# Routed attention with a GELU block on one core: the row-sum check one turn later, and operands of later batches prepared closer to their use

## The chip, the core and the metric

One core of a Trainium2 chip runs the whole program. The metric is device time in microseconds (us). Engines are named as in the profile: PE is TensorE (PEld its weight loads), DVE is VectorE, ACT is ScalarE, POOL is GpSimd, SP issues most DMAs. L409 is line 409 of the kernel before. Each engine takes its instructions strictly in the order in which the program writes them.

## The reference

For 4 batches, 8 heads, 768 positions and width 64, queries and keys are each given to the nearest of 16 centroids of their head; a query attends only to keys with the same centroid. The result goes through two matrix products with a quick GELU between them.

```
q_assign = np.argmax(np.einsum('bhsd,hcd->bhsc', q_n, c_n), axis=-1)
k_assign = np.argmax(np.einsum('bhsd,hcd->bhsc', k_n, c_n), axis=-1)
mask = q_assign[:, :, :, None] == k_assign[:, :, None, :]
scores = np.where(mask, scale * np.matmul(q, k.transpose(0, 1, 3, 2)), -1e9)
attn = softmax(scores);  x = (attn @ v) as (B*S, H*D) = (3072, 512)
h = x @ w_in                      # 512 -> 2048
out = (h * sigmoid(1.702 * h)) @ w_out
```

The arrays come as 64-bit floats. q, k and v are read as 32-bit; the two weight matrices are rounded on the chip.

## The kernel before

**Units and turns.** The heads are taken in pairs: 16 pairs p, four to a batch. A group g is one pair and one half (384) of its queries; groups run batch by batch, first half of the queries for pairs 0 to 3, then second half. A group has six units u, one for each 128 keys. The main loop runs over turns t of two units each: three turns to a group, 24 to a batch, 96 turns and two more to drain. Scheduling is manual: what the loop writes is the order on every engine.

**One turn** writes, in this order:

1. `scores(u)` (L384, PE) for its two units into two PSUM buffers `s`; for batch 0 `part(u)` (L398) adds the mask by a small matmul. Both `s` buffers must have been released by the exponentials of the turn before.
2. `exps(u)` (L409, ACT).
3. From turn 12 on (`second`), one `round_next()`.
4. `mask(u)`: DVE L420 from batch 1 on; POOL adds the exponentials up in `sum` (L430).
5. `prep_near` of a pair, where it is due; then `values(u)` (L441, PE) for the units of the turn before, and at a group's end a copy of the result to `x` (L446, ACT).
6. In every third turn (4, 7, 10, ...) `normalise(g)`: ones matmul over `sum` (L453, PE), reciprocal (L456, DVE), product with x (L458, DVE). From turn 12 on it stands ahead of the other preparation steps, before that behind them.
7. The other preparation steps of this turn.
8. `check(g)`: two ACT passes over the reciprocals (L468, L470), whose row sums tell at the end whether this fast path was valid. It overwrites the reciprocals, so it waits for L458.
9. `round_next()` in most turns; then pieces of the second block; and in odd turns from 12 on one more `round_next()`.

**Rounding of weights.** 32 pieces of 128x512 come by DMA (`raw`, 512 KB, three buffers, L146). A round has two DVE operations (L159, L161), two of ACT on their results (L163, L165), and three more of DVE for the piece before (L171, L174, L177). Rounds run in turns 1 to 21; before turn 12 none is written at the end of turns 3, 7 and 11.

**Preparation of a pair** has seven steps, one for a turn in batches 1 to 3 and two for a turn in batch 0:

- steps 0 to 3, `prep_turn`: three transposes (L262, PE) into a PSUM bank, and a copy to `T` (L267, ACT). Step 0 also loads v (L120); steps 1 and 3 also take the next q or k load from a queue (L111, three buffers).
- step 4, `prep_near`: four small matmuls (L276) and a copy (L282, ACT).
- step 5, `prep_assign`: transposes (L287, PE) and five DVE operations (L293 to L316).
- step 6, `prep_spread`: one transpose (L323), a copy (L328, ACT), and two DMAs (L330, L332) that spread the codes to all partitions as `qb`. For batch 0 this step is `prep_hot` (L349, with evictions L354 and L356).

**The second block** for a half batch is 16 `first` (four 128x128 by 384 products, each written as two passes, L487; tanh L492 on ACT; product L494 on DVE) and then 12 `second` (four products, L504; every fourth one evicts `y`, L510, ACT, and stores it). They are taken at a rate of about 2.4 for a turn from turn 14 on. All short PSUM tiles of preparation, normalisation and second block (`m`) share three banks; a `y` holds one of them over several pieces.

The lines that place the steps of later batches:

```
            elif b == 0:
                t = (hp - 2) * TG + 1 + i // 2
            else:
                t = b * TB + (-20, -8, -2, 1)[hp] + i
            prep_at.setdefault(t, []).append((p, i))
```

Of the kernel before, what the change touches and what calls it, by code (L numbers as in the profile page):

```python
# [18 lines left out]
def kernel(  # L19
    tc: tile.TileContext,  # L20
    q: bass.AP,
    k: bass.AP,
    v: bass.AP,
    centroids: bass.AP,
    moe_w_in: bass.AP,
    moe_w_out: bass.AP,
    out: bass.AP,
):

    args = (q, k, v, centroids, moe_w_in, moe_w_out, out)
    bad = fast(tc, *args)
    with tc.If(bad > 0):
        general(tc, *args)
# [3 lines left out]
def fast(  # L39
# [142 lines left out]
    def round_next():  # L182
        i = w_done[0]
        if i < NW:
            load_w(i + 2)
            split_w(i)
        if 0 < i <= NW:
            join_w(i - 1)
        w_done[0] += 1
# [183 lines left out]
    def split(g):  # L373
        b, r = divmod(g, 2 * HP)
        h, hp = divmod(r, HP)
        return b * HP + hp, h

    def scores(u):
        g, kt = divmod(u, NJ)
        p, h = split(g)  # L380
        ps = ps_s.tile([P, 2, 512], FP32, name="s")
        for a in range(2):
            rows = slice(a * D, (a + 1) * D)
            nc.tensor.matmul(out=ps[:, a, 0:HALF],  # L384
                             lhsT=T[p, 1][rows, kt * P:(kt + 1) * P],
                             rhs=T[p, 0][rows, h * HALF:(h + 1) * HALF],
                             start=True, stop=(p >= HP))
        s_of[u] = ps[:, :, 0:HALF]

    def part(u):  # L390

        g, kt = divmod(u, NJ)
        p, h = split(g)
        if p >= HP:
            return
        for a in range(2):
            r = 32 * (2 * (p % 2) + a)
            nc.tensor.matmul(  # L398
                out=s_of[u][:, a, :],
                lhsT=hots[p // 2, 1][r:r + NC, kt * P:(kt + 1) * P],  # L400
                rhs=hots[p // 2, 0][r:r + NC, h * HALF:(h + 1) * HALF],
                start=False, stop=True)

    def exps(u):
        p, h = split(u // NJ)
        s = s_of[u]
        if p < HP:
            A_of[u] = ap.tile([P, 2, HALF], FP32, name="A")
        nc.scalar.activation(out=A_of[u] if p < HP else s, in_=s, func=AF.Exp,  # L409
                             scale=SCALE)  # L410

    def mask(u):

        g, kt = divmod(u, NJ)
        p, h = split(g)
        s = s_of.pop(u)
        if p >= HP:
            A_of[u] = ap.tile([P, 2, HALF], FP32, name="A")
            for a in range(2):
                nc.vector.scalar_tensor_tensor(  # L420
                    out=A_of[u][:, a, :],
                    in0=qcode[p][:, a, h * HALF:(h + 1) * HALF],
                    scalar=code[p][:, kt % NH, 1, kt // NH, a:a + 1],
                    in1=s[:, a, :], op0=ALU.is_equal, op1=ALU.mult)
        A = A_of[u]
        if kt == 0:
            return
        if kt == 1:
            sum_of[g] = ap.tile([P, 2, HALF], FP32, name="sum", bufs=2)
        nc.gpsimd.tensor_tensor(out=sum_of[g],  # L430
                                in0=A_of[u - 1] if kt == 1 else sum_of[g],
                                in1=A, op=ALU.add)

    def values(u):
        g, kt = divmod(u, NJ)
        p, h = split(g)
        if kt == 0:
            o_of[g] = ps_o.tile([P, 512], FP32, name="o")
        A = A_of.pop(u)
        for a in range(2):  # L440
            nc.tensor.matmul(out=o_of[g][a * D:(a + 1) * D, 0:HALF],  # L441
                             lhsT=v_in[p][:, a, kt, :], rhs=A[:, a, :],
                             start=(kt == 0), stop=(kt == NJ - 1))
        if kt == NJ - 1:
            O_of[g] = xp.tile([P, HALF], FP32, name="x")
            nc.scalar.copy(O_of[g], o_of.pop(g)[:, 0:HALF])  # L446

    def normalise(g):

        sm = sum_of.pop(g)  # L450
        ps = bank()
        for a in range(2):
            nc.tensor.matmul(out=ps[a * D:(a + 1) * D, 0:HALF], lhsT=ones,  # L453
                             rhs=sm[:, a, :], start=True, stop=True)
        rec = recs[g] = short()
        nc.vector.reciprocal(out=rec, in_=ps[:, 0:HALF])  # L456
        x = xT_of[g] = O_of.pop(g)
        nc.vector.tensor_tensor(out=x, in0=x, in1=rec, op=ALU.mult)  # L458
        if g % HP == HP - 1:
            ffn.extend(ffn_chunks(g // HP))  # L460

    recs = {}

    def check(g):


        rec = recs.pop(g)
        nc.scalar.activation(out=rec, in_=rec, func=AF.Copy,  # L468
                             accum_out=sums[:, 0, g:g + 1])
        nc.scalar.activation(out=rec, in_=rec, func=AF.Relu, bias=top[:, 0:1],  # L470
                             scale=-2.0 * LIMIT * LIMIT,
                             accum_out=sums[:, 1, g:g + 1])
# [51 lines left out]
    TB = 2 * HP * TG  # L524

    prep_at = {}
    for p in range(1, NPAIR):
        b, hp = divmod(p, HP)
        for i in range(2 if p == 1 else 0, len(PREP)):
            if p == 1:  # L530
                t = (i - 2) // 2
            elif b == 0:
                t = (hp - 2) * TG + 1 + i // 2
            else:
                t = b * TB + (-20, -8, -2, 1)[hp] + i
            prep_at.setdefault(t, []).append((p, i))
    loads = deque((p, w) for p in range(NPAIR) for w in range(2))
    for _ in range(3):
# [2 lines left out]
    def prep(p, i):  # L541
        if i == 0 and p:
            load_v(p)
        PREP[i](p)
        if i in (1, 3) and loads:
            load_qk(*loads.popleft())
# [7 lines left out]
    for t in range(NT + 2):  # L554
        us = range(2 * t, 2 * t + 2) if t < NT else ()
        for u in us:
            scores(u)
        if t == 0:
            prep(0, 6)
        for u in us:  # L560
            part(u)
        for u in us:
            exps(u)
        second = t >= TB // 2
        if second:
            round_next()
        for u in us:
            mask(u)
        work = sorted(prep_at.get(t, ()), key=lambda w: PREP[w[1]] != prep_near)
        while work and PREP[work[0][1]] == prep_near:  # L570
            prep(*work.pop(0))
        if 1 <= t <= NT:
            for u in range(2 * t - 2, 2 * t):
                values(u)
        owed = owed + rate if ffn else 0.0
        g = (t - 2) // TG if t >= 2 and (t - 2) % TG == TG - 1 else None
        if g is not None and second:
            normalise(g)
        for p, i in work:
            prep(p, i)  # L580
        if g is not None and not second:
            normalise(g)
        if recs:
            check(*recs)
        if second or t and t % 4 != 3:
            round_next()
        while owed >= 1 and ffn:
            ffn.popleft()()
            owed -= 1
        if second and t % 2:  # L590
            round_next()


    ok = const.tile([P, 2, 2 * NPAIR], FP32, name="ok")
    nc.vector.tensor_scalar(out=ok, in0=sums, scalar1=LIMIT, scalar2=None,
# [457 lines left out]
```

## Time and profile before

| | us |
|---|---|
| median of 3 runs (1087.89 to 1088.94) | 1088.09 |
| profiled execution | 1089.2 |
| its span, first to last instruction | 1087.3 |
| PE busy / DVE / ACT / POOL in the span | 1049.0 / 490.8 / 354.8 / 296.9 |
| ACT idle until L458 ahead of L468 (32 times) | 111.2 |
| PE idle until L409 ahead of L384 (5 times) | 9.6 |

Lines of the timeline give start, duration, engine, line, operation, output and input, shapes and count; in brackets stands the idle time of the engine before it, and who ended it. Neighbouring instructions of one form are merged. Turns are found by their scores: turn 4 starts on PE at 34.80 us, turn 10 at 69.33, turn 12 at 82.10, turn 16 at 118.78, turn 20 at 168.65, turn 25 at 229.57, turn 46 at 450.54.

### The profile page before, as it was taken

Reading aid. Unit: us, or ns where it says so; the run is one execution under the profiler, and the core shown is the slowest. Engines: PE = TensorE matmul, PEld = TensorE weight load, DVE = VectorE, ACT = ScalarE, POOL = GpSimd, SP = SyncE. Lnnn points to the kernel's source line nnn. Section 1 sums busy time; section 2 is a strip of 40 time slices with the busy share of each in tenths; the row PEclk is TensorE's granted clock in tenths of the full one; section 3 lists DMA queues with packets and bytes.
Section 4 is the critical chain, followed back from the end, with each engine's and each line's share of the span. In section 5 each row is a group of like instructions: output and inputs, shape, how many; then the busy total and the mean of one; then the engine's idle time right before and its main releaser. Section 6 shows DMA issues by size and latency. Waiting matters only on the chain. (4 is left out here: it accounts for less than half of the span.)

```text
span 1087.3 us, 10456 instructions
## 1 busy us (share of the span) xinstructions
PE 1049.0 (96%) x3982; PEld 492.6 (45%) x3982; DVE 490.8 (45%) x744; ACT 354.8 (33%) x665; POOL 296.9 (27%) x168
## 2 busy tenths in 40 slices
PE   7878799999999999999999999999999999999997
PEld 3423344445544455444454445444554445444543
DVE  3889999225442344424453164423552344431200
ACT  3755555223422333223432233223332133311100
POOL 2644223213232333123231142222332333230000
PEclk9998899999999999999999999999999999999999
DMA  7623443110100010002100000010000000000000
GB/s 199 165 81 116 131 133 111 46 49 17 49 23 27 10 30 15 31 25 54 51 23 17 15 20 15 15 48 32 8 7 12 10 10 1 1 10 20 1 11 22
DMA packets 64813, 45.13 MB, mean 42 GB/s; under 512 B 51953, under 2 KB 57585, under 8 KB 64753
## 3 DMA queue, kind: packets, MB, share of 16 engines
q1 hardware_dynamic: 64608, 44.33, 14.3%
q8 instruction: 33, 0.54, 0.2%
q14 instruction: 28, 0.22, 0.1%
q10 hardware_dynamic: 144, 0.03, 0.0%
HBM read 38.04 MB, written 6.31 MB: 41 GB/s over the span
## 5 line engine op out<-in xcount | busy, mean ns | idle before, releaser
L430 POOL TENSOR_TENSOR sum<-sum,A 128x768 f32<-128x768 f32 x128 | 235.5, 1840 | 461.3 <-DVE A L420 364.1
L487 PE MATMUL m<-x,w_in 128*128 128x384 f32 x1024 | 347.1, 494 | 9.7 <-ACT T L267 4.4
L504 PE MATMUL m<-w_out,g 128*128 128x512 f32 x768 | 337.8, 594 | 0.7 <-ACT short L282 0.7
L420 DVE SCALAR_TENSOR_TENSOR A<-qb,code,s 128x384 f32<-128x384 uint8 x288 | 157.6, 609 | 274.6 <-ACT s L409 251.9
L487 PEld LDWEIGHTS m<-x,w_in 128*128 128x128 f32 x1024 | 192.2, 192 | 149.1 <-issue 16.3
L504 PEld LDWEIGHTS m<-w_out,g 128*128 128x128 f32 x768 | 143.3, 190 | 175.6 <-issue 171.5
L494 DVE SCALAR_TENSOR_TENSOR g<-g,m 128x384 f32<-128x384 f32 x128 | 70.0, 553 | 220.4 <-ACT g L492 220.3
L384 PE MATMUL s<-T,T 64*128 64x384 f32 x768 | 152.9, 517 | 9.7 <-ACT A L409 9.6
L409 ACT ACTIVATE s<-s 128x768 f32<-128x768 f32 x144 | 107.9, 792 | 136.0 <-PE s L384 136.0
L441 PE MATMUL o<-A,inv 128*64 128x384 f32 x768 | 146.3, 502 | 0.0
L492 ACT ACTIVATE g<-m 128x384 f32<-128x384 f32 x128 | 61.7, 487 | 196.4 <-PE m L487 196.3
L430 POOL TENSOR_TENSOR sum<-A 128x768 f32<-128x768 f32 x32 | 60.0, 1876 | 215.6 <-DVE A L420 179.5
L384 PEld LDWEIGHTS s<-T,T 64*128 64x128 f32 x768 | 66.6, 189 | 94.6 <-issue 52.2
L456 DVE RECIPROCAL short<-m 128x384 f32<-128x384 f32 x32 | 81.6, 2551 | 25.8 <-PE m L453 25.8
L441 PEld LDWEIGHTS o<-A,inv 128*64 128x64 f32 x768 | 46.8, 137 | 84.8 <-issue 84.1
L510 ACT ACTIVATE y<-m 128x512 f32<-128x512 f32 x24 | 14.3, 595 | 155.8 <-PE m L504 142.7
L468 ACT ACTIVATE short<-short 128x384 f32<-128x384 f32 x32 | 16.7, 523 | 111.2 <-DVE x L458 111.2
L409 ACT ACTIVATE A<-s 128x768 f32<-128x768 f32 x48 | 36.1, 804 | 22.0 <-PE s L398 22.0
L267 ACT COPY T<-m 128x384 f32<-128x384 f32 x64 | 29.7, 480 | 37.2 <-PE m L262 37.1
L262 PE MATMUL m<-ident,in 128*128 128x128 f32 x192 | 33.9, 298 | 3.1 <-ACT T L267 1.7
L163 ACT ACTIVATE e<-e,low 128x512 int32<-128x512 int32 x32 | 23.1, 722 | 28.8 <-DVE e L159 28.8
L262 PEld LDWEIGHTS m<-ident,in 128*128 128x128 f32 x192 | 21.5, 146 | 22.4 <-issue 11.9
(68 smaller groups left out, 373.5 us busy)
## 6 DMA issues: line engine op xcount, KB each, us to landing
raw<-in_moe_w_in_dram SPq DMA_DIRECT2D x16, 512.0 KB
raw<-in_moe_w_out_dram SPq DMA_DIRECT2D x16, 512.0 KB
in<-in_q_dram SPq DMA_DIRECT2D x32, 192.0 KB
in<-in_k_dram SPq DMA_DIRECT2D x32, 192.0 KB
inv<-in_v_dram SPq DMA_DIRECT2D x16, 384.0 KB
out_dram<-y SPq DMA_DIRECT2D x24, 256.0 KB
qb<-line SPq DMA_DIRECT2D x12, 192.0 KB
line<-row SPq DMA_DIRECT2D x12, 1.5 KB
```

The costliest lines, as they stand in the source:

```text
L262: nc.tensor.transpose(out=ps[:, n * P:(n + 1) * P], in_=qk_in[p, w][:, h * NH + n].rearrange("p a d -> p (a d)"), identity=ident)
L267: nc.scalar.copy(dst, ps[:, 0:HALF])
L384: nc.tensor.matmul(out=ps[:, a, 0:HALF], lhsT=T[p, 1][rows, kt * P:(kt + 1) * P], rhs=T[p, 0][rows, h * HALF:(h + 1) * HALF], start=True, ...
L409: nc.scalar.activation(out=A_of[u] if p < HP else s, in_=s, func=AF.Exp, scale=SCALE)
L420: nc.vector.scalar_tensor_tensor(out=A_of[u][:, a, :], in0=qcode[p][:, a, h * HALF:(h + 1) * HALF], scalar=code[p][:, kt % NH, 1, kt // NH ...
L430: nc.gpsimd.tensor_tensor(out=sum_of[g], in0=A_of[u - 1] if kt == 1 else sum_of[g], in1=A, op=ALU.add)
L441: nc.tensor.matmul(out=o_of[g][a * D:(a + 1) * D, 0:HALF], lhsT=v_in[p][:, a, kt, :], rhs=A[:, a, :], start=(kt == 0), stop=(kt == NJ - 1))
L456: nc.vector.reciprocal(out=rec, in_=ps[:, 0:HALF])
L487: nc.tensor.matmul(out=ps[:, 0:HALF], lhsT=w_in[:, c, f * P:(f + 1) * P], rhs=xT[c], start=(c == 0), stop=(c == NCH - 1))
L492: nc.scalar.activation(out=g, in_=ps[:, 0:HALF], func=AF.Tanh, scale=0.851)
L494: nc.vector.scalar_tensor_tensor(out=g, in0=g, scalar=1.0, in1=ps[:, 0:HALF], op0=ALU.add, op1=ALU.mult)
L504: nc.tensor.matmul(out=ps[:, 0:DM], lhsT=hs[f][:, n * P:(n + 1) * P], rhs=w_out[:, f, :], start=(f == 0), stop=(f == NF - 1))
```

## The change

Two edits. First, `check(g)` no longer stands at the end of the turn in which the group was normalised, but in the next turn, directly behind its exponentials and ahead of its first round; after the loop one call is left for the last group. Second, the steps of the first two pairs of batches 1, 2 and 3 are written later: step i of the first pair in turn 24b-8+i instead of 24b-20+i, of the second pair in turn 24b-5+i instead of 24b-8+i. The third and fourth stay. No operation is added or left out.

```
-                t = b * TB + (-20, -8, -2, 1)[hp] + i
+                t = b * TB + (-8, -5, -2, 1)[hp] + i
...
         for u in us:
             exps(u)
+        if recs:
+            check(*recs)
         second = t >= TB // 2
         if second:
             round_next()
...
         if g is not None and not second:
             normalise(g)
-        if recs:
-            check(*recs)
         if second or t and t % 4 != 3:
             round_next()
...
         if second and t % 2:
             round_next()
 
+    check(*recs)
```

So pair 4, the first of batch 1, is prepared in turns 16 to 22 instead of 4 to 10, and pair 5 in turns 19 to 25 instead of 16 to 22. For pairs 8 and 12 it is the same 12 turns, for pairs 9 and 13 the same 3 turns.

More of the change, by code (lines that the diff above doesn't have):

```diff
@@ L534, in fast @@
             else:
-                t = b * TB + (-20, -8, -2, 1)[hp] + i
+                t = b * TB + (-8, -5, -2, 1)[hp] + i
             prep_at.setdefault(t, []).append((p, i))
@@ L563, in fast @@
             exps(u)
+        if recs:
+            check(*recs)
         second = t >= TB // 2
@@ L582, in fast @@
             normalise(g)
-        if recs:
-            check(*recs)
         if second or t and t % 4 != 3:
@@ L591, in fast @@
             round_next()
+    check(*recs)
     ok = const.tile([P, 2, 2 * NPAIR], FP32, name="ok")
```

## The prediction

> **What bounds the kernel now.** I read the page first, then the stretches of 10 us, the waits of ACT and PE, and the timelines at the places that these name. The page: engine totals, and the rows of 40 slices.
>
> ```profile
> PE 1049.0 (96%) x3982; PEld 492.6 (45%) x3982; DVE 490.8 (45%) x744; ACT 354.8 (33%) x665; POOL 296.9 (27%) x168
> ...
> PE   7878799999999999999999999999999999999997
> PEclk9998899999999999999999999999999999999999
> ```
>
> PE is the bound, and from slice 6 on it leaves no room: whatever is saved there on ACT or DVE is worth nothing. Only the first 130 us have holes, and they have another owner. The stretches (us, then busy time of PE, PEld, DVE, ACT, POOL):
>
> ```profile
> 70.00:80.00 10.00, 7.19 (x43) 2.27 (x39) 9.73 (x14) 3.87 (x8) 4.88 (x3) 1.00 0.23 68
> 120.00:130.00 10.00, 6.03 (x31) 2.61 (x27) 9.93 (x14) 5.65 (x11) 3.70 (x2) 0.96 0.33 105
> 140.00:150.00 10.00, 10.00 (x47) 4.89 (x49) 9.93 (x14) 5.89 (x11) 3.99 (x2) 1.00 0.51 141
> ```
>
> From 70 to 131 us DVE (rounds and reciprocals) is full and PE is not; from 131 us PE is full. PE's holes from 40 to 131 us add up to 20.8 us; those from 140 to 1000 us to only 3.7. The waits of ACT, then of PE:
>
> ```profile
> ACT short L468 <- DVE x L458: 111.2, 32, 10.6
> PE s L384 <- ACT A L409: 9.6, 5, 4.0
> PE m L487 <- ACT T L267: 4.4, 3, 4.1
> ```
>
> ACT loses 111 us to the check, but PE feels the exponentials that queue behind it in five turns, all of batch 0, for 9.6 us.
>
> **Edit 1, the check.** One of the five, turn 10 to 12 (ACT, DVE and PE timelines):
>
> ```profile
> 78.87 0.53 ACT L468 ACTIVATE short<-short 128x384 f32<-128x384 f32 x1 [3.47 <-DVE x L458]
> 80.13 0.71 ACT L163 ACTIVATE e<-e,low 128x512 int32<-128x512 int32 x1
> 81.26 1.49 ACT L409 ACTIVATE A<-s 128x768 f32<-128x768 f32 x2
> 77.43 1.40 DVE L458 TENSOR_TENSOR x<-x,short 128x384 f32<-128x384 f32 x1
> 78.75 0.41 DVE L159 TENSOR_SCALAR e<-raw 128x512 int32<-128x512 int32 x1
> 82.10 2.93 PE L384 MATMUL s<-T,T 64*128 64x384 f32 x8 [4.00 <-ACT A L409]
> ```
>
> Taken away, the check uncovers the next wait: L163 of the round needs L159, which stands on DVE right behind L458 and ends at 79.16. L163 could start then instead of 80.13: the edit by itself is worth 1.0 us here, not 4. Turn 4 to 5 is the same (44.74 instead of 45.70), and there the check, 1.26 us of ACT, then stands between exponentials and the T copies (L267) on which PE's L276 of turn 6 waits; I keep 0.3 us. Only behind turn 7, which has no round, does the whole wait go. From turn 13 on, ACT's rounds wait for DVE anyway (1.6 us before the L163 that follows the exponentials of turns 14 and 20, 2.3 a round later in turn 17), and the check's 1.26 us fits there. In batches 1 to 3 PE waits for nothing behind a check: 0 on both sides; were that cover gone, a 1.26 us check ahead of L282 or a T copy would cost at most those 1.26 us.
>
> **Edit 2, what leaves turns 4 to 10.** Pair 4 costs PE 4 x 0.38 (three transposes; start to start at 222.23 and 222.61) + 0.79 (L276) + 0.38 (L287) + 0.15 (L323) = 2.85 us; ACT 4 x 0.48 + 0.48 + 0.25; DVE 2.74 us, from here to L159 at 72.17:
>
> ```profile
> 69.43 0.56 DVE L293 TENSOR_REDUCE best<-m 128x24 f32<-128x384 f32 x1 [3.52 <-PE m L287]
> 74.78 2.55 DVE L456 RECIPROCAL short<-m 128x384 f32<-128x384 f32 x1
> ```
>
> DVE's idle 3.52 us ahead of it goes too, and the 1.05 us at 60.07 (L453 waited 1.37 us for a bank that pair 4 no longer takes). I follow the queues with these durations. Turn 7's L456 starts at 58.7 (60.07 - 1.05 - 0.3). Exponentials of turn 8 start at 60.1 instead of 64.59; the check of turn 7's group follows at 62, the round's L163 and L165 end at 64.9, exponentials of turn 9 run then (67.47 before), so scores of turn 10 start at 65.7 (69.33), L453 ends at 70.0, and turn 10's L456 starts there instead of 74.78: 4.8 us earlier. DVE was ready at 67.3 and now waits for PE. From 74.78 to 131 us DVE idles 0.61 us in all, so what it gains it keeps to the end of the stretch: I take 5.0 us. The upper end is all DVE idle time of 40 to 70 us and the work: 2.03 + 0.25 + 1.05 + 3.52 + 2.74 = 9.6. The lower end: POOL's adds slow DVE. L174 takes 0.69 us, and 2.31 beside the add that starts at 47.76; the two adds at 65.52 ran while DVE was idle, and would now stand beside the rounds of turns 8 and 9: 2 x 1.62 less, 1.8 us. I stay near the middle, since the idle at 67.3 absorbs one. The raw loads keep pace: the one row that shows a wait for them (106.11) landed 3.9 us after its buffer came free, and the shortest lead in my replay is about 4.4.
>
> [...]
>
> **Where the 2.85 us go.** To turns 16 to 25, where PE is full: +2.85 us. So the early stretch nets -5.0 + 2.85 = -2.15. DVE's assign step falls in turn 21 as pair 5's did. For batches 2 and 3 the same work moves from full turns to full turns: 0. Of the moved DMAs, v waits for nothing new; pair 4's and 5's `qb` is spread two turns, about 20 us, ahead of its masks, as for pairs 6, 7, 10 and 11, where no wait shows: 0. One q or k load more stands between the raw loads of turns 17 to 20; a late piece would cost about one 0.61 us wait.
>
> **What two pairs at once cost.** Three turns now hold steps of two pairs that held one, and the three banks are the price (PE at turns 20, 22 and 25, then ACT):
>
> ```profile
> 172.80 5.43 PE L487 MATMUL m<-x,w_in 128*128 128x384 f32 x16
> 178.90 3.70 PE L504 MATMUL m<-w_out,g 128*128 128x512 f32 x8 [0.67 <-ACT short L282]
> 197.81 0.55 PE L262 MATMUL m<-ident,in 128*128 128x128 f32 x3 [0.34 <-ACT row L328]
> 234.27 0.55 PE L262 MATMUL m<-ident,in 128*128 128x128 f32 x3 [0.57 <-ACT T L267]
> 178.38 0.46 ACT L282 COPY short<-m 128x384 f32<-128x384 f32 x1
> ```
>
> While a `y` holds one bank and the normalisation another, each further step waits for the eviction before it. Turn 22 held a spread and one turn step (0.34); it gets a second turn step: +0.57. Turn 25 held two turn steps (0.57); it gets a spread ahead: +0.34. The same in turns 46, 49, 70, 73, where the profile shows the same two gaps: 3 x 0.91 = +2.7 us, surest of all terms. Turns 19, 43, 67 get two turn steps without a `y`; the like in turn 28 showed 0.2, which goes: +0.1 each, 0.3.
>
> Turn 20 is the costly one. ACT reaches L282 only at 178.38, behind a round whose DVE half is slowed. PE went on with two `first` until 178.2 and lost 0.67. Now T(5,1) takes the bank of the second `first`, which must wait for L282: PE is through with 0.38 + 2.65 us of work at 175.9 and stands until 178.9, 3.0 us instead of 0.67: +2.3. Between 0 (if the round isn't slowed, L282 comes at 175.5) and 3.8: a hole of 2.94 us ahead of 114.47 was followed by eight L487 in 4.38 us instead of 2.85, 1.5 us of slow clock.
>
> [...]
>
> **Sum.** -5.0 + 2.85 + 2.7 + 0.3 + 2.3 = +3.2 us (rounded): span 1087.3 to 1090.5, profiled execution 1089.2 to 1092.4. The median of the runs is 1.1 below the profiled execution, so 1088.1 + 3.2 = 1091.3.
>
> **Rivals.** (a) The early stretch wins, faster. PE's 9.6 us behind the exponentials go whole, and with the 4.00 us hole its slow clock, 1.37 + 0.32 + 1.27 = 3.0 us (rows at 82.10, 84.97, 85.72); less 2.85 moved and the 5.3 of banks put back: -9.6 - 3.0 + 8.2 = -4.4, 1083.7. It decides if turn 12's scores start before 74 us, that is, if DVE is not what PE waits for next. Against it stands DVE at 9.9 of 10 from 80 to 130 us. (b) Nothing moves: the early gain is 7 to 8 us and cancels the banks, or turn 20 stays as it was: 1087 to 1090. (c) Worse: DVE gains only 1.8 us, turn 20 costs 3.8 with slow clock: -1.8 + 2.85 + 3.0 + 3.8 = +7.9, 1096.0.
>
> **How the numbers follow.** Forecast case (+1 to +6): 0.57; (a) 0.15; (b) 0.20; (c) 0.08. The range may leave out two thirds of (a), 0.10, and most of (c), 0.06, and a little of the forecast case: 1085.0 to 1094.8. About 0.2% (2.2 us) can be told from no change. Faster by more: (a), 0.15. Within: (b) and 0.10 of the forecast case that lies below +2.2, 0.30. Slower: 0.55.
>
> **What would show it.** Right: DVE's L456 of turn 10 near 70 us, PE full from about 126 us, gaps of 0.3 and 0.6 both in turns 22, 25, 46, 49, 70, 73, one of 2 to 3 us in turn 20. Wrong: full PE before 122 us, or no second gap in those six turns. ACT's wait ahead of L468 should fall from 111.2 to under 10 us in every case, and says nothing of the time.

## The result, and the profile after

| | before | changed |
|---|---|---|
| median of 6 runs (lowest to highest) | 1087.87 us (1086.88 to 1088.94) | 1093.32 us (1091.79 to 1094.15) |
| span of the profiled execution | 1087.3 us | 1090.0 us |

The ratio is 1.0049, with a 95% interval of 1.0036 to 1.0062: 5.4 us slower. Run again beside the experiments with few adds, the changed kernel gave 1092.53 us and 1.0041 (1.0025 to 1.0058).

The two spans are only 2.7 us apart, because the profiled execution after began better: turn 5 starts on PE at 38.14 us there, against 41.06 before. Three transposes gone from turn 4 explain 0.4 us of that. The rest belongs to the execution, not to the change: in the twelve executions profiled for this study, turn 5 began between 37.95 and 41.10 us. So below all traces are laid over each other at the start of turn 5. From there to the last turn the changed kernel loses 5.57 us; less the 0.38 us already gained in turn 4 that is 5.2, which agrees with the medians.

The page of the changed kernel, engine totals and the slices of PE:

```profile
PE 1046.7 (96%) x3982; PEld 492.4 (45%) x3982; DVE 495.1 (45%) x744; ACT 354.6 (33%) x665; POOL 294.1 (27%) x168
...
PE   7887799999999999999999999999999999999997
```

Still PE from slice 6 on. DVE has the same 744 instructions and is busy for 4.3 us more; that is the trail to the early stretch. The three stretches that were shown of before:

```profile
70.00:80.00 10.00, 7.73 (x50) 2.80 (x46) 8.90 (x10) 5.54 (x11) 6.66 (x4) 1.00 0.35 105
120.00:130.00 10.00, 5.66 (x14) 2.90 (x13) 9.90 (x10) 3.27 (x6) 3.68 (x2) 0.85 0.40 136
140.00:150.00 10.00, 10.00 (x43) 5.10 (x43) 9.90 (x17) 6.70 (x12) 1.97 (x2) 1.00 0.43 127
```

DVE is full up to 130 us as it was, but for the first stretch (8.90 instead of 9.73). The waits of ACT and PE:

```profile
ACT short L468 <- DVE x L458: 4.5, 4, 1.3
PE s L384 <- ACT A L409: 9.5, 5, 2.7
PE m L487 <- ACT short L282: 1.7, 1, 1.7
```

The check's 111.2 us of ACT are down to 4.5, and PE's wait for exponentials went from 9.6 to 9.5. The place that the prediction showed, turns 10 to 12, now reads (ACT, DVE, PE):

```profile
74.99 0.72 ACT L163 ACTIVATE e<-e,low 128x512 int32<-128x512 int32 x1 [4.33 <-DVE e L159]
76.14 1.49 ACT L409 ACTIVATE A<-s 128x768 f32<-128x768 f32 x2
71.40 2.56 DVE L456 RECIPROCAL short<-m 128x384 f32<-128x384 f32 x1 [0.96 <-PE m L453]
74.54 0.42 DVE L159 TENSOR_SCALAR e<-raw 128x512 int32<-128x512 int32 x1
76.98 1.62 PE L384 MATMUL s<-T,T 64*128 64x384 f32 x8 [2.27 <-ACT A L409]
```

ACT no longer waits for L458 but for L159, next on DVE: a wait of 4.33 us stands where one of 3.47 was. PE's hole is 2.27 us instead of 4.00, and others have grown.

**Where the time went, by turns** (start of a turn on PE, both traces set to zero at turn 5):

| turns | changed less before, us | what is in it |
|---|---|---|
| 5 to 17 | -2.35 | pair 4's work gone, DVE 1.1 earlier at turn 16; 1.3 is a shorter slow clock behind the hole of turn 16 (before: granted clock 0.50 from 130 to 136 us, sixteen passes of L487 in 8.38 us; at 172.80 us, at 1.00, in 5.43) |
| 17 to 26 | +5.32 | pair 4's 2.85; turn 20's hole +1.1; turn 19's +0.24; turns 22 and 25 +0.91; 0.2 not placed |
| 26 to 43 | -2.95 | pair 8's work leaves turns 28 to 34 |
| 43 to 50 | +4.24 | it comes back; +0.24, +0.91 |
| 50 to 74 | +1.30 | the same for pair 12 |
| 74 to 95 | 0.0 | |

The 1.3 us of clock are not shown to be the change's. Four profiled executions share the changed program up to turn 17: two of the changed kernel, and those of the experiments batch1_only and offset6 below. In three of them the sixteen passes behind that hole took 7.12 us, in offset6 8.29, nearly the 8.38 of before; there turns 5 to 17 gain only 1.27 us. What is alike in all four is that the hole ends 1.1 to 1.3 us earlier than before, counted from turn 5.

PE's gaps in turns 20, 22 and 25 of the changed kernel:

```profile
173.25 2.85 PE L487 MATMUL m<-x,w_in 128*128 128x384 f32 x8 [1.75 <-ACT short L282]
195.07 0.55 PE L262 MATMUL m<-ident,in 128*128 128x128 f32 x3 [0.34 <-ACT row L328]
196.18 0.55 PE L262 MATMUL m<-ident,in 128*128 128x128 f32 x3 [0.57 <-ACT T L267]
233.20 0.55 PE L262 MATMUL m<-ident,in 128*128 128x128 f32 x3 [0.34 <-ACT row L328]
234.32 0.55 PE L262 MATMUL m<-ident,in 128*128 128x128 f32 x3 [0.57 <-ACT T L267]
```

### The profile page after: what moved, and what is told of

Read it like the earlier page. It is cut to its first block, busy times and chain, and to the rows that moved or that the text cites. A ratio compares the mean times of both kernels' runs of the same rounds, so it can differ in the third digit from the quotient of the medians.

```text
span 1090.0 us, 10516 instructions
## 1 busy us (share of the span) xinstructions
PE 1046.7 (96%) x3982; PEld 492.4 (45%) x3982; DVE 495.1 (45%) x744; ACT 354.6 (33%) x665; POOL 294.1 (27%) x168
## 5 line engine op out<-in xcount | busy, mean ns | idle before, releaser
L487 PE MATMUL m<-x,w_in 128*128 128x384 f32 x1024 | 347.9, 495 | 13.2 <-ACT T L267 5.1
L487 PEld LDWEIGHTS m<-x,w_in 128*128 128x128 f32 x1024 | 192.5, 192 | 153.2 <-issue 15.0
L384 PE MATMUL s<-T,T 64*128 64x384 f32 x768 | 151.6, 513 | 9.5 <-ACT A L409 9.5
L492 ACT ACTIVATE g<-m 128x384 f32<-128x384 f32 x128 | 62.3, 490 | 240.2 <-PE m L487 240.2
L384 PEld LDWEIGHTS s<-T,T 64*128 64x128 f32 x768 | 65.9, 187 | 93.4 <-issue 52.8
L456 DVE RECIPROCAL short<-m 128x384 f32<-128x384 f32 x32 | 81.7, 2552 | 25.7 <-PE m L453 25.6
L163 ACT ACTIVATE e<-e,low 128x512 int32<-128x512 int32 x32 | 23.1, 723 | 48.9 <-DVE e L159 48.8
L171 DVE SCALAR_TENSOR_TENSOR e<-raw,e 128x512 int32<-128x512 int32 x32 | 26.7, 836 | 0.0
```

Of the source, the lines that this page charges most:

```text
L384: nc.tensor.matmul(out=ps[:, a, 0:HALF], lhsT=T[p, 1][rows, kt * P:(kt + 1) * P], rhs=T[p, 0][rows, h * HALF:(h + 1) * HALF], start=True, ...
L487: nc.tensor.matmul(out=ps[:, 0:HALF], lhsT=w_in[:, c, f * P:(f + 1) * P], rhs=xT[c], start=(c == 0), stop=(c == NCH - 1))
L492: nc.scalar.activation(out=g, in_=ps[:, 0:HALF], func=AF.Tanh, scale=0.851)
```

## The experiments

Two theories were to be told apart. The ledger (A): the early stretch gains little, since freed exponentials put POOL's adds beside DVE's rounds, and the loss is moved PE work and bank waits. Against it (B): the later check itself does harm.

**Each edit alone.** The check alone:

```
-                t = b * TB + (-8, -5, -2, 1)[hp] + i
+                t = b * TB + (-20, -8, -2, 1)[hp] + i      # in the changed kernel
```

> The check one turn later, operands placed as in the kernel before. Theory A (a ledger: the early stretch gains little, since the freed exponentials put POOL's adds beside DVE's rounds; the loss is moved PE work and bank waits, all of the second edit): -1.0 us against the kernel before, between -2.5 and 0; no new PE waits in turns 19 to 25 and 46 to 73. Theory B (the later check itself hurts, because its 1.26 us of ACT now stand ahead of copies on which PE waits): +1 to +3 us. Theory C (the prediction's own size of the gain, 5 us of which about half came from the check): -2.5 to -5.

Measured: 1087.63 against 1087.81 us, ratio 0.9999 (0.9991 to 1.0008). No gain and no loss; between turn 5 and the last turn its trace lies 0.2 us behind the kernel before. B falls, and so does a gain of 2.5 us or more. A's range held it, but nearer its end of no gain than its -1.0.

The later placing alone (the same line, the other way, in the kernel before):

> The later placing of operands, check where it was before. Theory A: about +6 us against the kernel before (changed kernel +5.4, and without the check's gain of about 1), between +5 and +8; the same pairs of gaps of 0.34 and 0.57 us in turns 22, 25, 46, 49, 70, 73. Theory B: +2 to +4, the rest of the +5.4 being the check's.

Measured: 1096.15 us, ratio 1.0080 (1.0061 to 1.0099), 8.3 us. B is out: without the later check the placing costs more, not less. It lies just above A's range of +5 to +8, and the trace shows where extra time comes from: turn 20 (PE, then the stretch of 175 to 180 us).

```profile
174.39 4.26 PE L487 MATMUL m<-x,w_in 128*128 128x384 f32 x8 [2.13 <-ACT short L282]
175.00:180.00 5.00, 5.00 (x10) 2.43 (x10) 4.06 (x9) 2.11 (x4) 0.00 (x0) 0.66 0.95 255
```

With the check at the end of turn 19 on ACT, L282 starts 8.9 us after the start of turn 20 instead of 8.5: the hole is 2.13 us instead of 1.75, and after it the granted clock is 0.66 for five microseconds and eight passes take 4.26 us instead of 2.85. Turn 20 is 2.1 us longer than in the changed kernel (turn starts 164.98 to 182.29, against 164.23 to 179.46). So the check's new place is worth nothing by itself and, by this pair of traces, about 2 us beside the second edit: 0.4 of hole, the rest mostly slow clock. The clock is seen in one execution here; the medians put the whole at about 3 us.

**Only batch 1** (batch1_only).

```
-                t = b * TB + (-8, -5, -2, 1)[hp] + i
+                t = b * TB + ((-8, -5, -2, 1) if b == 1 else (-20, -8, -2, 1))[hp] + i
```

> The changed kernel, with the pairs of batches 2 and 3 placed as in the kernel before. Theory A: the two later batches cost 2 x 0.91 us of bank waits and some 0.2, so about 2.0 us below the changed kernel, +3.4 against the kernel before. Rival: all of the loss lies in batch 1 (moved work and turn 20), later batches are neutral: +5.4.

Measured: 1091.56 us, ratio 1.0038 (1.0023 to 1.0053), +3.8 us. The interval, +2.5 to +5.8 us, holds the rival's +5.4 too; the trace decides. From turn 26 to the last turn its trace neither gains nor loses against the kernel before (0.0), where the changed kernel loses 2.6. The later batches are not neutral.

**The three banks** (offset6). One turn between the two pairs more:

```
-                t = b * TB + (-8, -5, -2, 1)[hp] + i
+                t = b * TB + (-8, -6, -2, 1)[hp] + i
```

> The changed kernel, with the second pair of batches 1 to 3 one turn earlier (6 turns ahead instead of 5), so that no turn holds normalisation, a spread and two transposing steps. Theory A (three banks): the second gap goes in all six turns, 2.7 us below the changed kernel, +2.7 against the kernel before; turn 20 keeps its gap of 1 to 2 us. Rival (the cost is the density of preparation as such, or the later DMAs): no more than 0.5 us below the changed kernel.

Measured: 1090.44 us, ratio 1.0022 (1.0013 to 1.0030), +2.6 us where 2.7 was expected. By the trace the match is partly luck: from turn 17 on it lies 3.6 us below the changed kernel's, 1.2 for each batch where 0.91 was counted, and it had lost 1.1 us against it before turn 17, by the clock named above. PE's waits between 440 and 510 us are those of the kernel before:

```profile
PE m L262 <- ACT T L267: 0.6, 1, 0.6
PE m L262 <- ACT row L328: 0.3, 1, 0.3
```

In the changed kernel the same stretch has two of each, 1.1 and 0.7 us. The density of preparation stayed the same; only what meets a normalisation changed.

**POOL's adds.** In both kernels the adds of batch 0 were cut to the first of each group:

```
-        if kt == 0:
+        if kt == 0 or p < HP and kt > 1:
             return
```

> The kernel before without POOL's last four adds of each group of batch 0 (they are left out: the row sums of that batch take two of six key tiles). Theory A (POOL's adds hold DVE's rounds): DVE's slow forms (about 2.0 and 2.3 us) in the stretch of 40 to 131 us become few, DVE is through with it earlier, and the kernel gains 5 to 12 us. Rival (DVE's slow forms have another cause, such as DMA or ACT): under 2 us.

> The changed kernel with the same adds left out. Theory A: with the adds gone the change's early gain is no longer eaten, so this one stands closer to the one without the change than the +5.4 us with all adds: +1 to +3 us between the two (-5.0 early instead of -1.5). Rival (the early gain is limited by DVE's own work or by the DMA of the weights, not by adds): the difference stays +5 to +6.

> The changed kernel as it is, for comparison on this chip: +5.4 us against the kernel before, between +4.5 and +6.5, in both theories.

Measured, beside 1087.31 us of the kernel before: 1074.07 us (0.9875, 0.9854 to 0.9896) for the kernel before with few adds, 1072.47 us (0.9865, 0.9844 to 0.9887) for the changed one with few adds, 1092.53 us for the changed kernel as it is. The 32 adds left out cost the kernel before 13 us, a little more than the range. Without them the 5.2 us between the two vanish: the changed one is 1.6 us ahead by the medians, though the ranges overlap, and level by the traces (0.4 us behind from turn 5 on, less the 0.38 of turn 4). That is below the range of +1 to +3; the direction is A's.

The groups of the rounds show it: duration of all and mean ns, in the changed kernel first, then with few adds.

```profile
L159 DVE TENSOR_SCALAR e<-raw 128x512 int32<-128x512 int32 x32 | 25.5, 796 | 0.8 <-DMA raw<-in_moe_w_in_dram 0.7
L161 DVE TENSOR_SCALAR w_in<-raw 128x512 int32<-128x512 int32 x16 | 16.5, 1029 | 0.0
```

```profile
L159 DVE TENSOR_SCALAR e<-raw 128x512 int32<-128x512 int32 x32 | 13.5, 422 | 1.5 <-DMA raw<-in_moe_w_in_dram 1.1 <-DMA raw<-in_moe_w_out_dram 0.2
L161 DVE TENSOR_SCALAR w_in<-raw 128x512 int32<-128x512 int32 x16 | 6.8, 426 | 0.0
```

And DVE's stretch from the reciprocal of turn 4 to that of turn 16 adds up (from the timelines; "slow" is what L159 to L177, L299 and L458 took above 0.42, 0.69, 0.36 and 0.56 us, where that is over 0.11 us):

| us | whole | work | slow | idle |
|---|---|---|---|---|
| before | 89.7 | 64.6 | 19.7 (14 times) | 5.4 |
| changed | 88.6 | 62.3 | 23.5 (16 times) | 2.8 |
| before, few adds | 78.9 | 64.6 | 3.0 (3) | 11.3 |
| changed, few adds | 72.4 | 62.6 | 4.3 (3) | 5.5 |

The change takes 4.9 us of work and idle time from DVE. Of that, 3.8 come back as slow instructions, and 1.1 us is left. With few adds it takes 7.8, of which 1.4 come back, and 6.4 are left. The other traces tell which edit does it: the check alone has 23.6 us of slow time and 2.6 of idle, the later placing alone 23.1 and 3.3. So either edit by itself fills DVE's pauses with held instructions, and a check alone that gains nothing fits that.

**A version that beats both.** If the gaps are a matter of what meets a normalisation, the kernel before has some to give as well (0.34 in turns 22, 46, 70 and 0.57 in 25, 49, 73):

```
-                t = b * TB + (-8, -5, -2, 1)[hp] + i
+                t = b * TB + (-20, -9, -3, 1)[hp] + i      # apart_9_3
+                t = b * TB + (-20, -6, -3, 1)[hp] + i      # apart_6_3; ..._early: check as before
```

> The check as in the changed kernel; the pairs of batches 1 to 3 placed 20, 9, 3 turns ahead and 1 after (instead of 20, 8, 2 in the kernel before), so that no turn with a normalisation holds two preparing steps that need a bank ahead of the second block. Theory A (three banks): both gaps of the kernel before (0.34 in turns 22, 46, 70 and 0.57 in turns 25, 49, 73) go as well, 3 x 0.91 = 2.7 us below the kernel before, less about 0.2 for the check: -2.5 us; batch 1's first steps in turns 15 to 18, beside rounds, add 0 to 1. Rival (a step costs its gap wherever it stands): no more than 0.5 us below the kernel before.

> The same with the second pair 6 turns ahead instead of 9. Theory A: the same 2.7 us, and in batch 1 turn 16 has no transposing step whose copy waits behind a slowed round (4.1 to 4.3 us of PE in the runs so far; other banks are held by the normalisation and the second block, so I count only 1 to 2 us of it); turn 20 gets such a step beside the second pair's and keeps or loses its gap (0.7): -3 to -4.5 us against the kernel before. Rival: under 0.5 us below it.

> The placing of the run before this one, with the check where it is in the kernel before. If the check's place is worth nothing by itself (0 in the run with the check alone): within 1 us of that run. If it is worth something only where preparation stands beside rounds, as the runs with and without it suggest (2 to 3 us): 1 to 3 us slower.

Measured, beside 1088.38 us: 1085.43 us (0.9976, 0.9967 to 0.9985), 1086.24 us (0.9981, 0.9972 to 0.9990) and 1086.88 us (0.9988, 0.9979 to 0.9997). All are faster than the kernel before, the first by 2.6 us by the ratio (3.0 by the medians) where 2.5 was expected; no preparing transpose waits for a bank any more from turn 26 on, and turns 36 to 60 and 60 to 84, which hold the preparation of the later pairs of batches 2 and 3, are 1.15 to 1.38 us shorter each. The second missed its -3 to -4.5: batch 1 moved its holes instead of losing them. In turn 16 PE then waited 5.22 us for the normalisation's bank (L456 on DVE) where it had waited 4.09 for T's copy. In the first, turns 15 and 20 have:

```profile
113.83 8.34 PE L487 MATMUL m<-x,w_in 128*128 128x384 f32 x16 [5.24 <-DVE g L494]
179.22 3.67 PE L504 MATMUL m<-w_out,g 128*128 128x512 f32 x8 [2.39 <-DVE short L296]
```

The third came within 1 us of the second, as it should if the check's place is worth nothing by itself: 0.6 us by the medians, with intervals that overlap.

## Why the prediction was right, and which terms were not

The sign, the owners of the loss and the bank term held; the sum came out at +3.2 where 5.2 to 5.4 were measured. That it came so near is in part luck: the early gain was forecast 2.3 us too large, or more, and turn 20 1.2 us too dear, and the two partly cancel.

Of the prediction's four signs of being right, only the pairs of gaps in six turns were clearly met. DVE's L456 of turn 10 stands at 71.40 us and PE's last hole of the early stretch ends at 126.11, near the 70 and 126 that were named, but only because this execution began better; laid at turn 5 they are 74.3 and 129.0 on the clock of before. The gap of turn 20 is 1.75 us, not 2 to 3.

- **The check takes its wait to the next in the queue.** Right: L163 starts 0.03 us after L159's end, the exponentials of turn 11 follow at once, and the check alone measures 0, less than the 1.0 us at turn 10 that the prediction still gave it. ACT's 111.2 us fell to 4.5 without a gain, as the prediction said they would in every case.
- **The early stretch, -5.0: mis-sized; this is the step that failed.** "I stay near the middle, since the idle at 67.3 absorbs one" was wrong. The replay had scores of turn 10 start 3.6 us earlier; counted from turn 5 they came 0.7 earlier, and the reciprocal of turn 10, counted from that of turn 4, only 0.4 us earlier (33.2 instead of 33.6), not 4.8. The adds of turns 7 and 8 now run in one row from 56.23 to 63.99, and DVE's round stands in them:

```profile
60.28 2.04 DVE L159 TENSOR_SCALAR e<-raw 128x512 int32<-128x512 int32 x1
62.24 2.03 DVE L161 TENSOR_SCALAR w_in<-raw 128x512 int32<-128x512 int32 x1
56.23 7.76 POOL L430 TENSOR_TENSOR sum<-sum,A 128x768 f32<-128x768 f32 x4 [4.30 <-ACT A L409]
```

  By turn 17 the gain, with turn 4's 0.38, is 2.7 us, of which 1.3 is slow clock (sixteen passes in 7.12 us instead of 8.38) and so perhaps the execution's; without it 1.5 to 1.7 are left. The lower bound, 1.8 from the two adds, was nearer than the middle. The runs with few adds bear out the adds as the cause: L161's mean falls from 1029 to 426 ns. The 1.8 was worked out from L174, which reads two tensors; L159 and L161, held most often in the changed kernel (seven times each up to 150 us, at 1.58 to 2.05 us), read one.
- **The moved 2.85 us** came back whole: turns 28 to 35 of the changed kernel are 2.94 us shorter together, turns 43 to 50 longer by that and the gaps.
- **Two pairs at once, +2.7: right to the hundredth.** 0.34 and 0.57 us stand in all six turns, and one turn of distance removes one of each pair. For turns 19, 43, 67 I had 0.1 each; the trace has 0.24, and the later batches lose 1.3 us each where 1.0 was forecast.
- **Turn 20, +2.3: it is +1.1.** The hole is 1.75 us, not 3.0. PE did wait for L282, as forecast, but I had left ACT's queue as it was against PE: the exponentials of turn 20 start 2.9 us after their turn (4.2 before), and L282 8.5 (9.7 before).

```profile
172.74 0.46 ACT L282 COPY short<-m 128x384 f32<-128x384 f32 x1
```

  Of these 1.2 us the check's place gives 0.4 (L282 comes at 8.5 instead of 8.9 beside the later placing, and at 9.3 instead of 9.7 with the check alone). The other 0.8 come with the later placing, which makes turn 19 0.8 us longer on PE, so that turn 20 starts later against ACT. With the check in its old place the hole was 2.13 and the granted clock behind it 0.66: turn 20 was 3.4 us longer than before, near the 3.8 us of the upper bound.
- **The rivals.** (a) needed turn 12 before 74 us; it started at 76.98, in an execution that had begun 2.5 us better, and DVE was what PE waited for next. (b) needed an early gain of 7 to 8 us, or turn 20 as it was: the runs with few adds come near the gain, at 6.4 us and turn 4's 0.38, the changed kernel does not, and turn 20 grew. (c)'s early term was nearly the true one, its turn 20 was not.

## What to carry to other kernels

When a wait is taken out of one engine's queue, look at the instruction behind it: if that needs the same producer's next result, nothing was bought. Before idle time of an engine is counted as gain, ask what other engine's work will slide into it; here POOL's adds had run in DVE's pauses, and took 3.8 of the 4.9 us that were freed. And work moved "closer to its use" meets the buffers of that place: count which steps share a turn, not how many there are.

## What the runs showed of the hardware that was not expected

Thirty-two adds of one batch on POOL cost this kernel 13 us. Beside such an add, DVE's L159 and L161 took up to 2.05 us instead of 0.42, and L171, L174 and L177 up to 2.2 to 2.3 instead of 0.69. Its reciprocal from PSUM was never held: 2.54 to 2.56 us throughout, that of 74.78 us of before wholly beside the adds of 74.70 to 78.41. Once the delay fell on POOL: in the kernel before, L171 and L174 ran at 115.47 and 116.07 us in 0.71 us each, wholly inside an add, and that add took 3.25 us where one takes 1.84 in the mean:

```profile
115.19 3.25 POOL L430 TENSOR_TENSOR sum<-A 128x768 f32<-128x768 f32 x1 [6.07 <-ACT A L409]
```

The slow clock does not go by the length of PE's hole alone, and it differs between executions of one program. The changed kernel and offset6 write the same program up to turn 17. In both, PE's hole at turn 12 is 2.27 us; behind it the eight passes take 1.62 us in the changed kernel (at 76.98, shown above, at a granted clock of 1.00) and 2.81 us in offset6. The check alone and apart_9_3 write the same program up to turn 14; behind a hole of 3.08 us the first takes 2.93 us for the eight passes of L384, the second 1.62. Offset6, the check alone, apart_9_3:

```profile
79.23 2.81 PE L384 MATMUL s<-T,T 64*128 64x384 f32 x8 [2.27 <-ACT A L409]
81.03 2.93 PE L384 MATMUL s<-T,T 64*128 64x384 f32 x8 [3.08 <-ACT A L409]
80.44 1.62 PE L384 MATMUL s<-T,T 64*128 64x384 f32 x8 [3.08 <-ACT A L409]
```

Behind a hole of 2.13 us the clock was slow as well (the placing alone, turn 20: 0.66 from 175 to 180 us), behind one of 1.75 us in the changed kernel it stayed at 1.00 (170 to 180 us).
